# Ten more weight pairs as seven block products in a gated FFT + GEGLU kernel

## The chip, the cores and the metric

The kernel runs on one NeuronCore of a Trainium2 chip. A core has five engines that run their own instruction streams in order: PE (TensorE, matmuls), DVE (VectorE), ACT (ScalarE), POOL (GpSimd) and SP (SyncE). Transfers are issued from SP's and POOL's streams and run on 16 DMA engines. The metric is the device time of the one core in microseconds (us).

## The reference

The input is one sequence of 2048 tokens with 576 features. Two branches are mixed by a gate that is one number per token:

```python
g = sigmoid((x * gate_w).sum(-1, keepdims=True))
a = irfft2(rfft2(A_x) * (w_r + 1j * w_i))        # over tokens and features
h = gelu_tanh(B_x @ w_gate) * (B_x @ w_up)       # 576 -> 4608
b = h @ w_down                                   # 4608 -> 576
out = g * a + (1 - g) * b
```

All is float32. In the drawn inputs A_x and B_x hold the same values, so that the kernel reads one x.

## The kernel before, in words

**GEGLU branch.** Tokens are taken in two halves of 1024, and the 4608 hidden features in 36 blocks of 128; two blocks are a pair, so that there are 2 x 18 = 36 pairs to do. The matmul type is the reduced-precision float32r; to keep accuracy every operand is split into a high part (a rounded copy, made by ACT) and a low part (value minus high, made by DVE), and a product is the sum of high x high, low x high and high x low.

In the convolution form ("c", the functions `chain` and `hidden`) a block times 512 tokens is a chain of 14 matmuls of 512 columns: four feature slices of three matmuls (lines 726 to 728) and two for the last, stacked slice (lines 732 and 733). Gate and up weights make two chains, ACT takes gelu of the first, DVE multiplies by the second, and the result is split (`hb`).

In the block-product form ("s", the function `products`) a pair of blocks times 1024 tokens is treated as a 2 x 2 block product and computed with seven block products instead of eight (the Strassen-Winograd scheme). The x side is summed and split once (`operands`, into the tiles `sx` and `s4`). On the weight side four quarter blocks are loaded (`load_b`), subtracted by DVE (line 949) and split (`prep_b`, line 957). Each product is two groups of seven matmuls of 512 columns (`seven`, lines 972 to 975). DVE adds the products (line 1007) before gelu and multiplication.

In both forms the down projection (`down_mm`, line 787) has 12 matmuls of 288 columns for 128 tokens and a pair, 96 per pair and half. ACT evicts each sum, scaled by 1 - g, into one of four staging tiles (`put`, line 812), and POOL adds it to the DRAM rows `yd` with an accumulating transfer (line 800).

**Spectral branch.** The 2-D transform is done beside this, almost all on DVE: row transforms along the 576 features for each half (`forward_rows`: nine-point step, three radix-4 stages, twiddles), token transforms between tiles (`first_tiles`), the column stage (`columns`) with its own matmuls of 290 columns, the filter, and the way back (`last_tiles`, `inverse_rows`). The scaled rows are accumulated into `yd` by POOL. The 16 spectral tiles fill one large tile `til` (37 KB a partition); the operands `sx` use the same place once the tiles are gone.

**Order.** Each engine's order is written out by the program. After each half chain, each group of seven and each down sum, `gap()` is called: it issues what has fallen due (`at(n, ...)` puts a step n gaps later, `seq` a row of such steps, `due` forces the rest of a row out before its result is used), then one entry of the start list `aux`, and then steps of the spectral generator as long as a credit is positive. Matmuls raise the credit by their estimated time times `RATE` (`tick`), DVE steps lower it by their estimated duration, and a step that yields `None` ends the gap. So the spectral work is spread over the matmuls at the pace of the credit.

The 36 pairs are: 18 c pairs for the first half; for the second half five c pairs and then 13 s pairs, once the inverse transform is over and `operands` is done. Chains write to two PSUM banks (`pgu`); the column stage holds two others (`pf2`), which become `pone` for the s pairs.

Of the kernel before, what the change touches and what calls it, by code (L numbers as in the profile page):

```python
# [29 lines left out]
RATE = 1.02  # L30
STEP = 6
FIRST = 5
# [125 lines left out]
def _build(nc, tc, a):  # L158
    with ExitStack() as ctx:
# [3 lines left out]
        spec = ExitStack()  # L163
        psf = spec.enter_context(tc.tile_pool(name="psf", bufs=1, space=bass.MemoryType.PSUM))
# [12 lines left out]
        til = mk("til", [16 * SW])  # L177
        gu = [mk(f"gu{i}", [2, KT, 256], F32R) for i in range(3)]
        dn = [mk(f"dn{i}", [2, D], F32R) for i in range(4)]
        raws = mk("raws", [2 * (KT * 256 + D)])  # L180
        raw = [raws[:, i * (KT * 256 + D):(i + 1) * (KT * 256 + D)] for i in range(2)]
        hb = [mk(f"hb{i}", [2, TB], F32R) for i in range(3)]
        gl = [mk(f"gl{i}", [TB]) for i in range(2)]
        xraw = mk("xraw", [4, TB])
        stg = [mk(f"stg{i}", [2, HD]) for i in range(4)]
        tmp = mk("tmp", [2 * UNIT + 112])
        sgn = tmp[:, 2 * UNIT + 112 - KF:]
# [4 lines left out]
        cns = mk("cns", [4, NK])  # L192
        misc = mk("misc", [2 * SW])
        gwb = misc[:, 0:D]
# [9 lines left out]
        def ps_f2():  # L204
            return psf.tile([P, 2, 512], F32, name="pf2", tag="pf2", bufs=1)

        ps7 = []

        def ps_one():
            return ps7[0].tile([P, TB], F32, name="pone", tag="pone", bufs=2)  # L210
# [9 lines left out]
        st = [til[:, SW * i:SW * (i + 1)] for i in range(16)]  # L220
# [9 lines left out]
        def columns():  # L230
# [5 lines left out]
            Z = [st[q] for q in turn]  # L236
            flat = xraw.rearrange("p q k -> p (q k)")
            sp, gw, xg = flat[:, 0:SW], flat[:, SW:SW + D], flat[:, 1280:1280 + D]
# [30 lines left out]
            def product(d, kb, h, l):  # L269
                v = ps_f2()  # L270
                c = cc(d, kb).rearrange("p (a l k) -> p a l k", a=2, l=2)
                for al in range(2):
                    for n, (q, x) in enumerate(((0, h), (1, h), (0, l))):
                        pe.matmul(v[:, al, :NK], c[:, al, q], two(x)[:, al], start=n == 0, stop=n == 2)  # L274
# [6 lines left out]
            def gates():  # L281

                nc.sync.dma_start(gw, a["gw"][0:1, :].to_broadcast([P, D]))
                for t in range(8):
                    n = count[0]
                    at(2, lambda t=t: nc.sync.dma_start(xg, a["xg"][t]))
                    while count[0] < n + 7:
                        yield None
                    gate_sum(8 + t, xg, xg, gw)
                    yield 1.33  # L290
                gate_part(1, None)[1]()

            def beside():

                more = gates()
# [3 lines left out]
                for d in range(3):  # L299
                    while gone[0] < (4 * d + 5) * STEP + 5:  # L300
                        yield next(more, None)
                    yield from four(d, range(4), sp, 1)
                yield from more
# [18 lines left out]
            for kb in range(18):  # L322
# [5 lines left out]
                def filter_start():  # L328
                    vec.tensor_tensor(zi, v[:, 0, :NK], zr, ALU.subtract)
                    vec.tensor_tensor(zr, v[:, 0, :NK], zr, ALU.add)  # L330
# [10 lines left out]
                for g in range(STEP):  # L341
# [9 lines left out]
                    elif g == 1:  # L351
                        if on:
                            copy(zr, v[:, 1, :NK])
# [14 lines left out]
                    elif g == 4:  # L368
                        if was:
                            w = product(1, kb - 1, yh, yl)  # L370
                            copy(two(Z[kb - 1]), w[:, :, :NK])
# [19 lines left out]
        T = til.rearrange("p (e d k) -> p d e k", d=4, e=4)  # L391
        re, im = slice(0, NK), slice(NK, SW)

        def four(d, at, sp, sgn):

            yield from _butterfly(vec, lambda i: T[:, d, i], lambda i: T[:, d, i, re], lambda i: T[:, d, i, im],
                                  at, sp, sgn, (0.76, 0.45))

        def first_tiles(h):

# [5 lines left out]
                                  TAKEN, sp, -1, (1.37, 0.76))  # L406
            places = [((k, TAKEN[o]), o * k) for k in range(1, 4) for o in range(1, 4) if TAKEN[o] // 2 == h]
            yield from _twiddles(vec, act, lambda d, e: T[:, d, e], lambda d, e: T[:, d, e, re],
                                 lambda d, e: T[:, d, e, im], places, tmps, -1, 0.5)
            yield None  # L410

        def last_tiles():

# [6 lines left out]
                                 lambda d, e: T[:, d, e, im], places, tmps, 1, 0.5)  # L420
            yield None
            yield from _butterfly(vec, lambda i: T[:, i], lambda i: T[:, i, :, re], lambda i: T[:, i, :, im],
                                  range(4), sp, 1, (2.6, 1.35))
# [6 lines left out]
        def nine(ops):  # L430
            for o, x, c, z in ops:
# [8 lines left out]
                yield 0.45 if z is None else 0.72  # L440
# [827 lines left out]
```

## Time and profile before

| | |
|---|---|
| Three timed runs | 1386.92, 1387.72, 1387.68 us; median 1387.68 |
| Profiled execution | 1385.35 us, span 1383.5 us, granted TensorE clock 0.999 |
| Busy in the span | PE 1370.6, DVE 1038.4, ACT 752.7, POOL 266.1 us |
| DMA | 211.16 MB, mean 153 GB/s |

The profile page gives busy time per engine, the span in 40 slices (a digit is tenths of a slice), DMA queues, the chain of work that ended last, and groups of instructions by line. "PEld" is TensorE's weight load, which overlaps its matmuls. A wait row has: who waited <- for whom: total us, times, longest us. A group row has busy time and mean ns of one instruction, then the engine's idle time before them and what ended it. A row of a DMA issue has KB and the median time from issue to landing. Durations of matmuls overlap, since they are pipelined; their pace is read from the distance of their starts.

### The profile page before, as it was taken

Reading aid. Unit: us, or ns where it says so; the run is one execution under the profiler, and the core shown is the slowest. Engines: PE = TensorE matmul, PEld = TensorE weight load, DVE = VectorE, ACT = ScalarE, POOL = GpSimd, SP = SyncE. Lnnn points to the kernel's source line nnn. Section 1 sums busy time; section 2 is a strip of 40 time slices with the busy share of each in tenths; the row PEclk is TensorE's granted clock in tenths of the full one; section 3 lists DMA queues with packets and bytes.
Section 4 is the critical chain, followed back from the end, with each engine's and each line's share of the span. In section 5 each row is a group of like instructions: output and inputs, shape, how many; then the busy total and the mean of one; then the engine's idle time right before and its main releaser. Section 6 shows DMA issues by size and latency. Waiting matters only on the chain.

```text
span 1383.5 us, 19831 instructions
## 1 busy us (share of the span) xinstructions
PE 1370.6 (99%) x7504; PEld 1208.1 (87%) x7504; DVE 1038.4 (75%) x1440; ACT 752.7 (54%) x1215; POOL 266.1 (19%) x326
## 2 busy tenths in 40 slices
PE   8999999999999999999999999999999999999998
PEld 7888888888888888888888888888888888888888
DVE  5999899989878877799988997546555555555554
ACT  5553443444566575543456344866666666666662
POOL 0022111222222221111113012321112222221111
PEclk9999999999999999999999999999999999999999
DMA  7466666657899998556678467956677666766767
GB/s 269 144 123 115 154 121 122 115 100 172 207 248 268 253 256 177 103 106 117 144 140 184 117 143 136 205 81 162 131 131 132 130 129 128 132 130 130 131 138 180
DMA packets 97328, 211.16 MB, mean 153 GB/s; under 512 B 11856, under 2 KB 22096, under 8 KB 96848
## 3 DMA queue, kind: packets, MB, share of 16 engines
q0 software_dynamic: 45248, 92.56, 44.3%
q1 hardware_dynamic: 51984, 117.34, 27.0%
q8 instruction: 59, 0.97, 0.3%
q14 instruction: 37, 0.30, 0.1%
HBM read 110.69 MB, written 92.01 MB: 147 GB/s over the span
## 4 chain that ended last, share of the span: by engine, by line
PE 84%; issue 7%; DVE 4%; DMA 2%; POOL 1%; ACT 1%; SPq 1%; DVEq 0%; POOLq 0%; ACTq 0%
PE pdn L787 28%; PE pgu L726 10%; PE pgu L728 9%; PE pgu L727 9%; PE pgu L973 3%; PE pgu L972 3%; PE pgu L974 3%; PE pone L972 3%; PE pone L973 3%; PE pone L974 3%; PE pgu L732 2%; PE pgu L733 2%; PE pgu L975 2%; PE pf L274 2%; PE pone L975 1%
## 5 line engine op out<-in xcount | busy, mean ns | idle before, releaser
L800 POOL DMA_DIRECT2D yd<-stg x264 | 229.6, 871 | 1047.5 <-ACT stg L812 777.4
L787 PE MATMUL pdn<-dn,hb 128*128 128x288 f32 x2892 | 413.0, 295 | 0.0
L787 PEld LDWEIGHTS pdn<-dn,hb 128*128 128x128 f32 x2892 | 402.0, 188 | 11.8 <-DVE hb L773 0.2
L812 ACT ACTIVATE stg<-pdn,omg 128x576 f32<-128x576 f32 x272 | 201.7, 742 | 370.1 <-PE pdn L787 364.4
L726 PE MATMUL pgu<-xhi,gu 128*128 128x512 f32 x728 | 285.0, 392 | 5.0 <-DVE gl L768 3.4
L728 PE MATMUL pgu<-xlo,gu 128*128 128x512 f32 x728 | 284.0, 390 | 0.0
L727 PE MATMUL pgu<-xhi,gu 128*128 128x512 f32 x728 | 283.7, 390 | 0.0
L726 PEld LDWEIGHTS pgu<-xhi,gu 128*128 128x128 f32 x728 | 136.7, 188 | 31.4 <-DVE gl L768 5.0
L728 PEld LDWEIGHTS pgu<-xlo,gu 128*128 128x128 f32 x728 | 136.7, 188 | 29.8
L727 PEld LDWEIGHTS pgu<-xhi,gu 128*128 128x128 f32 x728 | 136.6, 188 | 24.5
L213 ACT ACTIVATE hb<-gl 128x512 fp32r<-128x512 f32 x102 | 64.0, 628 | 114.4 <-DVE gl L768 114.1
L213 ACT ACTIVATE gu<-raws 64x256 fp32r<-64x256 f32 (+3 forms) x121 | 101.6, 850 | 7.2 <-DMA raws<-wgu 5.7
L768 DVE TENSOR_TENSOR gl<-gl,pgu 128x512 f32<-128x512 f32 x92 | 62.9, 683 | 44.9 <-PE pgu L733 44.4
L764 ACT ACTIVATE gl<-pgu 128x512 f32<-128x512 f32 x91 | 54.3, 597 | 72.4 <-PE pgu L733 72.1
L787 PE MATMUL pdn<-dn,gu 128*128 128x288 f32 x540 | 83.6, 295 | 0.2 <-DVE raws L841 0.2
L787 PEld LDWEIGHTS pdn<-dn,gu 128*128 128x128 f32 x540 | 76.7, 188 | 1.9 <-DVE raws L841 0.5
L773 DVE TENSOR_TENSOR hb<-gl,hb 128x512 fp32r<-128x512 f32 x92 | 63.1, 686 | 16.5 <-ACT hb L213 16.5
L732 PE MATMUL pgu<-xtl,gu 128*128 128x512 f32 x182 | 70.9, 389 | 0.0
L733 PE MATMUL pgu<-xtl,gu 128*128 128x512 f32 x182 | 70.8, 389 | 0.0
L706 DVE TENSOR_TENSOR gu<-raws,gu 128x1280 fp32r<-128x1280 f32 x44 | 65.4, 1486 | 5.3 <-ACT gu L213 5.2
L706 DVE TENSOR_TENSOR dn<-raws,dn 128x576 fp32r<-128x576 f32 x72 | 54.1, 752 | 1.3 <-ACT dn L213 1.3
L92 DVE TENSOR_TENSOR rows<-rows 128x1280 f32<-128x1280 f32 x36 | 53.5, 1487 | 0.5
(232 smaller groups left out, 2137.0 us busy)
## 6 DMA issues: line engine op xcount, KB each, us to landing
yd<-stg POOLq DMA_DIRECT2D x264, 288.0 KB, 5.1
raws<-wgu SPq DMA_DIRECT2D x44, 640.0 KB, 5.0
raws<-wd SPq DMA_DIRECT2D x72, 288.0 KB, 3.2
colm<-col POOLq DMA_DIRECT2D x32, 256.0 KB, 6.3
raws<-ws SPq DMA_DIRECT2D x21, 384.0 KB, 6.6
quads<-ws SPq DMA_DIRECT2D x20, 384.0 KB, 6.8
tmp<-wf SPq DMA_DIRECT2D x16, 290.0 KB, 5.6
cns<-til SPq DMA_DIRECT2D x64, 72.5 KB, 5.1
```

The source lines that it names most:

```text
L213: act.activation(o, i, AF.Copy)
L706: vec.tensor_tensor(g[:, 1], r, f(g[:, 0]), ALU.subtract)
L726: pe.matmul(ps, w[:, 0, k, c], xhi[tb][:, k], start=k == 0, stop=False)
L727: pe.matmul(ps, w[:, 1, k, c], xhi[tb][:, k], start=False, stop=False)
L728: pe.matmul(ps, w[:, 0, k, c], xlo[tb][:, k], start=False, stop=False)
L732: pe.matmul(ps, w[:, 0, 4, c], xtl[tb], start=False, stop=False)
L733: pe.matmul(ps, w[:, 1, 4, c], xtl[tb], start=False, stop=True)
L787: pe.matmul(ps[half], h[:, l, c], d[:, q, half * HD:(half + 1) * HD], start=part == 0 and n == 0, stop=part == 1 and n == 2)
L800: pl.dma_start(yd[u], o, accum_op=ALU.add)
L812: put(u, lambda o: act.activation(o.rearrange("p (c k) -> p c k", c=2), v[:, :, 0:HD], AF.Copy, scale=omg[:, u:u + 1]), i == 0)
L972: pe.matmul(ps, hi, xh[:, t], start=start and t == 0, stop=False, skip_group_check=True)
L973: pe.matmul(ps, lo, xh[:, t], start=False, stop=False, skip_group_check=True)
```

## The change

The order of the pairs becomes a plan: 2 c, 10 s, 6 c for the first half, 5 c and 13 s for the second. So 23 pairs are block products instead of 13, in both halves, and what they need must exist twice.

- `operands` is called for each half. `sx` and the spectral tiles `til` take turns in one buffer: x, then `sx` of the first half, then `til` during the 11 c pairs, then `sx` of the second half. `s4` moves to a weight tile.
- While `sx` is there the rows of only one half fit in SBUF. Forward rows of half 0 are stored to DRAM (`fw`) and come back when the tiles exist; after the column stage the rows of half 1 are stored (`bw`) and come back for the last transform.
- The forward row transforms run in the first ten s pairs, the tile and column work in the c pairs, the inverse row transforms in the last 13 s pairs. `until` holds the generator for a phase; at the start of each s stretch the program issues gaps without matmuls until the operands are done, and before the last pair until the generator has ended.
- The weight quarters use five fixed places in turn instead of two sets of four; all are loaded from SP. The differences (`total`) are issued apart from the splits.
- Chains alternate between the banks `pgu` and `pone`, except in the column stage, which then uses `pone`. One more pair of hidden tiles comes from a tile `hx`.
- The credit has rate 1.0 instead of 1.02, a cap of 1.2 instead of 3.0, smaller charges for most DVE steps, and some charges are made at issue of the whole row of steps. The gates of half 1 are taken beside the first forward transform; sigmoid is written with tanh. Rows leave the inverse transform one by one. POOL's descriptor scratch is set to 4096 bytes.

```diff
-RATE = 1.02
+RATE = 1.0
 STEP = 6
-FIRST = 5
+PAIRS = NT // 2
+PLAN = "c" * 2 + "s" * 10 + "c" * 11 + "s" * 13
+PLACES = ((0, 1, 2), (2, 0, 1), (1, 2, 0))
...
+        fw, bw = (dram.tile([P, ROWS], F32, name=n, tag=n) for n in ("fw", "bw"))
...
-                yield 0.45 if z is None else 0.72
+                yield 0.36 if z is None else 0.61
...
-            yield from _butterfly(vec, *v, at, sp, sgn, (1.5, 0.82))
+            yield from _butterfly(vec, *v, at, sp, sgn, (1.41, 0.74))
...
+        def into_rows(h):
+
+            T = tile_view()
+            rows = rows_tile()
+            R = row_view(rows)
+            pl.memset(rows.rearrange("p (c k) -> p c k", c=2)[:, :, 8 * KF:], 0.0)
+            yield from moved(lambda t, c: (R[:, c, t, 0:KF], T[:, 8 * h + t, c, 0:KF]))
+            box[0] = rows
...
         def inverse_rows(h):
-            rows = rows_tile()
-            T, R = spread(h, rows)
...
+            rows = box[0]
...
+            todo_t = list(range(8))
+            n = 0
+            while todo_t:
+                t = min(todo_t, key=lambda t: abs(count[0] - added[8 * h + t] - 11)) if h else todo_t[0]
+                o = out_rows[n % 4]
+                n += 1
+                todo_t.remove(t)
+                act.activation(o, R[:, t, 0:D], AF.Copy, scale=gs[:, 8 * h + t:8 * h + t + 1])
+                at(2, lambda t=t, o=o: pl.dma_start(yd[8 * h + t], o, accum_op=ALU.add))
+                for _ in range(1 if n < 5 and h == 0 else 3):
+                    yield None
...
+        def until(n):
+            while phase[0] < n:
+                yield None
 
         def spectral(rows):
-            yield from forward_rows(0, rows)
+            yield from operands(0)
+            yield from with_gates(forward_rows(0, rows))
+            nc.sync.dma_start(fw, rows)
             rows = rows_tile()
             load_rows(rows, 1)
-            zero_pads(0)
+            for _ in range(9):
+                yield None
+            yield from forward_rows(1, rows)
+            yield from until(2)
+            til[0] = pool.tile([P, 16 * SW], F32, name="til", tag="til")
+            yield from into_tiles(1, rows)
+            rows = rows_tile()
+            nc.sync.dma_start(rows, fw)
+            yield from first_tiles(1)
+            yield from into_tiles(0, rows)
+            yield from first_tiles(0)
+            cols[0] = True
+            yield from columns()
+            cols[0] = False
+            yield from last_tiles()
+            load_xs(1, 0)
+            load_xs(1, 1)
+            yield from into_rows(1)
+            nc.sync.dma_start(bw, box[0])
             yield None
...
-            yield from columns()
-            yield from last_tiles()
-            for h in range(2):
-                yield from inverse_rows(h)
+            yield from into_rows(0)
+            yield from operands(1)
+            yield from until(3)
+            yield from inverse_rows(0)
+            box[0] = rows_tile()
+            nc.sync.dma_start(box[0], bw)
+            for _ in range(5):
+                yield None
+            yield from inverse_rows(1)
...
-            credit[0] = min(credit[0], 3.0)
+            credit[0] = min(credit[0], 1.2)
...
+        def bank():
+
+            turns[0] += 1
+            return ps_gu() if cols[0] or turns[0] // 2 % 2 else ps_one()
...
+        def load_b(q, n):
+            if q < len(PLAN) and PLAN[q] == "s":
+                nc.sync.dma_start(spots(q)[(0, 1, 3, 4)[n]], a["ws"][block(q, n // 2), n % 2])
...
-            seq(("b", i, m), (lead, total), (lead + 2, high), (lead + 4, low), (lead + 5, tail))
+            credit[0] -= 0.88
+            seq(("b", q, m), (lead + 1, high), (lead + 3, low), (lead + 4, tail))
...
+        for q, m in enumerate(PLAN):
+            current[0] = q
+            if q in starts:
+                while ops.get("done") != starts.index(q):
+                    credit[0] = 1.0
+                    gap()
+                phase[0] = 2 * starts.index(q) + 1
+            elif q and m == "c" and PLAN[q - 1] == "s":
+                phase[0] = 2
+            if q == len(PLAN) - 1:
+                while gens:
+                    credit[0] = 1.0
+                    gap()
+                for u in range(8):
+                    nc.sync.dma_start(a["y"][u], yd[u])
+            (conv if m == "c" else products)(q)
+        finale()
```

In `products` the order of the pieces within a pair is the same (seven products, down sums between them): weight loads for the next pair are issued after its second, third and fourth product, splits three products ahead of their use.

More of the change, by code (lines that the diff above doesn't have):

```diff
@@ L370, in columns @@
                             w = product(1, kb - 1, yh, yl)
[L371 removed]
+                            for al in range(2):
+                                copy(two(Z[kb - 1])[:, al], w[al][:, :NK])
                         if on:
@@ L814, in down, with pop @@
             gap()
+        def pop(n):
+            for _ in range(n):
+                if pend:
+                    d, t = pend.pop(0)
+                    down(d, t)
+                    if t == 3:
+                        spare.extend(u for _, u, _ in d[3])
+        pend = []
         def held(u):
-            return st[8 + u][:, 0:D]
+            return st(8 + u)[:, 0:D]
         def release(u):
```

582 lines of the change are left out of this document (292 added, 290 removed).

## Prediction

> **What bounds the kernel now.** I read the page first, then the busy time by stretches, the chain of waits, TensorE's waits, and DVE's instructions in order of time.
>
> ```profile
> span 1383.5 us, 19831 instructions
> PE 1370.6 (99%) x7504; PEld 1208.1 (87%) x7504; DVE 1038.4 (75%) x1440; ACT 752.7 (54%) x1215; POOL 266.1 (19%) x326
> DVE  5999899989878877799988997546555555555554
> ```
>
> TensorE is busy for all but 12.9 us of the span. DVE is near full in two thirds of the 40 slices and half idle in the last third, where the 13 block-product pairs run. The profiled execution took 1385.35 us (span 1383.5), 2.33 below the median of the three timed runs, 1387.68. I sum against 1385.35 and add 2.33 at the end.
>
> The chain of waits names the same group of 24 down matmuls twice in each pair. Its starts give the length of a pair, first for four convolution-form pairs ("c"), then for eleven product pairs ("s"):
>
> ```profile
> 183.41 3.18 PE pdn L787 x24
> ...
> 336.26 3.18 PE pdn L787 x24
> ...
> 965.28 3.18 PE pdn L787 x24
> ...
> 1351.24 3.18 PE pdn L787 x24
> ```
>
> A c pair takes (336.26 - 183.41) / 4 = 38.21 us, an s pair (1351.24 - 965.28) / 11 = 35.09 us. The same two stretches by engine (length, then PE, PEld, DVE, ACT, POOL, clock, DMA share, GB/s):
>
> ```profile
> 183.41:336.26 152.85, 152.85 (x835) 135.01 (x834) 137.44 (x185) 67.67 (x106) 30.10 (x37) 1.00 0.63 119
> 965.28:1351.24 385.96, 385.96 (x2137) 341.19 (x2136) 224.13 (x297) 240.20 (x418) 76.22 (x88) 1.00 0.69 130
> ```
>
> In both TensorE never rests and has full clock, so a matmul removed there is time removed. DVE is 90% busy in the first, with spectral work between the pairs; in the second, with an s pair's own work alone, 58% (20.4 us a pair). That free 42% is what the change wants to use.
>
> TensorE's waits, all that reach 0.4 us:
>
> ```profile
> PE pgu L726 <- DVE gl L768: 3.4, 3, 2.0
> PE pgu L726 <- ACT gl L761: 1.6, 1, 1.6
> PE pgu L1100 <- DVE gate L1096: 1.5, 1, 1.5
> PE pgu L745 <- DVE xhi L1106: 0.8, 1, 0.8
> ```
>
> **The change, part by part.**
>
> *Matmuls.* The plan string has 2 c, 10 s, 11 c and 13 s pairs: ten pairs turn from c to s. By the code a c pair has 8 chains of 14 matmuls of 512 columns, an s pair 7 products of 2 x 7, so 112 become 98. By the two spacings that is 10 x (38.21 - 35.09) = **-31.2 us**, all on TensorE's path.
>
> *DVE's ledger.* The spectral work is handed out by credit: matmuls earn (98 x 0.2265 + 96 x 0.131 = 34.8 in an s pair, 37.9 in a c pair), DVE work spends. The new charges are smaller than the old, 0.61 for 512 columns where the old had 0.72, 1.41 for 1280 where it had 1.5. DVE's order of time shows whether they are real:
>
> ```profile
> 209.91 0.69 DVE L435 TENSOR_TENSOR tmp<-rows 128x512 f32<-128x512 f32 x1
> 210.63 0.69 DVE L437 TENSOR_TENSOR rows<-rows 128x512 f32<-128x512 f32 x1
> 211.24 0.68 DVE L435 TENSOR_TENSOR tmp<-rows 128x512 f32<-128x512 f32 x1
> ...
> 220.51 1.49 DVE L92 TENSOR_TENSOR tmp<-rows 128x1280 f32<-128x1280 f32 x1
> 221.92 0.68 DVE L768 TENSOR_TENSOR gl<-gl,pgu 128x512 f32<-128x512 f32 x1
> ```
>
> An instruction lasts 0.69 us, but the next starts 0.61 us after it (210.63 to 211.24), or 0.72 where it reads what was just written (209.91 to 210.63). For 1280 columns it is 1.41. So the charges are the true pace of independent instructions; dependent ones run 0.11 over. About every second of the 31 instructions of the inverse nine-point step is such a one, and one or two in a stage: some 28 of its 94, so 28 x 0.11 = 3 us on 70 charged, 4%.
>
> An s pair charges 19.6 of its own: seven splits and four differences of weights at 0.88, six adds 3.7, four hidden blocks 4.9, two dn splits 1.4. That leaves 15.2 for spectral work; a c pair (9.1 of its own) leaves 28.9. Now stage by stage. First ten s pairs: the first has 8, the next nine 15.2 each, together 145; both forward row transforms with the gates want 80 + 73 = 153. The rest spills into the first c pair, which nothing forbids. The eleven c pairs: 0.55 pairs of spill; two moves into tiles 0.85; two first-tile steps 1.15; the column stage about 5.3 (107 gaps of its own pace, 24 gaps a pair, and what stands around it); last tiles 1.0; two moves into rows 0.8: 9.7 pairs, with 10 there before the operands of the second half must begin. Last 13 s pairs: two inverse transforms at 70.4 and some 45 gaps of idle pacing take 12 pairs, with 12 there. It fits, but nowhere with more than a third of a pair to spare.
>
> Where DVE is handed its full credit, its demand is 34.8 + 0.04 x 15.2 = 35.4 us per s pair against TensorE's 35.09: 0.3 us a pair over, for 18 such pairs 5.7 us. A split is issued two chains or more ahead of its use (8 us), so part of that is swallowed. Ends 0 and 15 (0.8 a pair); I take **+3**, between nothing and the whole of the 5.7.
>
> *Rows through DRAM.* Four transfers of 2560 KB are new. The nearest rows:
>
> ```profile
> rows<-xn SPq DMA_DIRECT2D x2, 2304.0 KB, 11.1
> raws<-ws SPq DMA_DIRECT2D x21, 384.0 KB, 6.6
> ```
>
> By size one takes about 11.1 x 2560 / 2304 = 12.3 us (estimate). After the first forward transform the rows are stored and the other half is loaded into the same buffer, so SP waits at that load for the store, 12.3 us, and the load takes 11.1 more: 23.4 us. The kernel waits nine gaps, and a gap of an s pair is 35.09 / 22 = 1.6 us: 14.4. DVE then stands for 9 us, and behind its first waiting instruction the pair's own adds and splits are queued. The 8 us of lead swallow most; what stays is lag in a stage where DVE can't catch up. Ends 0 and 9; I take **+4**, nearer the middle, since the lag isn't worked off before the c pairs. Weight loads stand behind this on SP's queue: the ledger puts the store in the last fifth of a pair, and the next loads are issued 8 us into the following one. They land at about their time; ends 0 and 12, taken as 0.
>
> [...]
>
> After the column stage the rows of half 1 are stored and those of half 0 moved into the same buffer one gap later. ACT's first copy comes some 3 us after the store is issued and waits for its end, about 9 us; the evictions of down sums stand behind it. The trace has a smaller case, ACT with 5.33 us of copies in one piece at 735, where TensorE waited the 2.0 us of the first wait row above:
>
> ```profile
> 735.42 5.33 ACT L580 ACTIVATE til<-rows,gs 128x576 f32<-128x576 f32 x4
> ```
>
> So about 3.3 us were swallowed with two banks for the chains. Now the chains have four outside the columns, two more chains of 3.2 us. Ends 0 (all swallowed) and 6 (9 - 3.3); I take **+3**. The burst itself goes, since rows now leave one by one: **-2**.
>
> The other two transfers: the load of the stored forward rows has 22 us of tile work before it is read (0). The last load has five gaps, 8 us, against 12.3; DVE stands for 4, within the lead (ends 0 and 4, taken 0).
>
> *Deadlines.* At each c-to-s change the program issues gaps without matmuls until the operands are done. Their generator needs about 27 gaps by its pauses and 18.6 us of charges at 1.2 a gap, and the pair before has 24 (the first time 23). The last three or four are issued at once: a few splits and eight 32-row copies, used only by the third product, 8 us on. Ends 0 and 6 each; **+1** each. The end rush before the last pair, at worst two row copies of the kind that took 5.33 / 4 = 1.3 us: **+1** (ends 0 and 4).
>
> *Costed at nothing.* The ACT work added (seven splits and seven 64-row copies a pair) has cover: ACT was busy 240.2 of 385.96 us in s pairs. Two 290-column copies instead of one in columns, the gates' loads moved to the first s pairs and tanh in place of sigmoid are ACT and SP work with the same cover; without it they cost under 3 us. The smaller descriptor scratch for POOL's transfers shows nowhere; by POOL's row (19% busy) even twice the issue time stays below the pairs' pace.
>
> Sum: 1385.35 - 31.2 + 3 + 4 + 3 - 2 + 2 + 1 = 1365.2; on the scale of the median 1367.5, so **1367**.
>
> **The rivals.**
>
> *All is covered.* Every new wait lies inside its lead: 1387.7 - 31.2 - 2 = 1354.5. For it: in 152.85 us with DVE 90% busy TensorE did not wait once. Against it: the full demand was under DVE's pace there, and it is over now.
>
> *SP's queue is the price.* If the forward transform ends in the first half of a pair, the weight loads of the next pair stand behind 23.4 us of rows. The first is used by ACT 9.5 us after issue and lands in 6.6 now; it would come 10 to 14 us late, and ACT's evictions behind it. That adds some 11 us to the forecast: 1378. Where the store falls hangs on the ledger, which I trust to 0.3 of a pair. [...]
>
> *The operands come late.* The c stage overruns by half a pair, and 12 gaps of operand work are issued with no matmul beside them, 10 us: 1377.
>
> *Slower: DVE sets the pace of s pairs.* In s pairs DVE now waits for ACT:
>
> ```profile
> DVE hb L995 <- ACT hb L213: 34.5, 19, 2.2
> DVE gl L991 <- ACT gl L999: 16.1, 13, 1.3
> DVE gu L995 <- ACT gu L213: 14.4, 7, 3.5
> DVE gu L957 <- ACT gu L213: 10.1, 25, 1.2
> ```
>
> That is 75.1 us over 13 pairs, 5.8 a pair. If half of it stays when DVE has no slack, each of 18 filled pairs is 2.9 us longer, 52 us: 1367 + 52 - 3 = 1416. It decides from (1387.7 - 1367.5 + 3) / 18 = 1.3 us a pair. Against it: DVE waits there because it runs ahead of the ACT copy that is issued with the matmuls; with work to do it comes later, and in the stretch at 183 no such wait reached TensorE.
>
> **How the numbers follow.** Forecast 0.55 (its own range 1358 to 1375), all covered 0.22, SP's queue 0.12, late operands 0.04, DVE's pace 0.07. A measurement of this kernel tells 0.2%, 2.8 us, from no change. Slower is the last rival, 0.07; same is the upper edge of the two before it, 0.03; faster 0.90. The range reaches down to the covered case with a little below, 1353, and up past SP's queue, 1382; the slower rival stays outside it.
>
> **What would show it.** Pairs of 35.1 us in 23 places and 14 matmuls of 512 columns fewer in each of ten pairs show the first term. TensorE waits of 2 to 6 us near 290 us (the store and load of rows) and near 800 (ACT waiting for the store of rows) show the next; none there means the covered case. S pairs of 35.4 to 36 with spectral work beside them show the ledger; above 36.4 the slower rival. Weights landing over 15 us after issue show SP's queue. I am wrong if TensorE's idle time outside start and end is over 30 us, or if the columns run into the last 13 pairs.

## The result

| | before | after |
|---|---|---|
| median of the runs | 1387.70 us | 1376.39 us (1374.25, 1377.17, 1376.51, 1376.27) |
| profiled execution, span | 1385.35, 1383.5 us | 1374.25, 1372.5 us |

The ratio is 0.9916, with an interval of 0.9899 to 0.9933. The change makes the kernel faster by 11.3 us, 0.8%; the forecast was 1367, a gain of 20.7, and its range (1353 to 1382) holds the time. So the sign is right, and nearly half of the expected gain went somewhere. These are the page's first rows for the kernel after, with DVE's and the clock's rows of the 40 slices:

```profile
span 1372.5 us, 20070 instructions
PE 1344.1 (98%) x7364; PEld 1186.9 (86%) x7364; DVE 1142.8 (83%) x1605; ACT 846.9 (62%) x1444; POOL 263.2 (19%) x322
...
DVE  7689999989999768867786587689989779989854
...
PEclk9999999999999999999999999989999999999999
```

TensorE has 140 matmuls fewer, and DVE is now 8 or 9 tenths full in most slices of both s stretches (4 to 13 and 27 to 38), where it had been half idle in the second. But TensorE stands for 28.4 us (1372.5 - 1344.1), where it stood for 12.9. The down groups of the chain of waits give the pairs as before, two starts of each stretch:

```profile
180.43 3.18 PE pdn L835 x24
215.48 3.18 PE pdn L835 x24
...
486.35 3.18 PE pdn L835 x24
524.56 3.18 PE pdn L835 x24
...
1106.01 3.18 PE pdn L835 x24
...
1316.33 3.18 PE pdn L835 x24
```

An s pair takes 35.05 us in the first half (215.48 - 180.43) and in the second (210.32 / 6), a c pair 38.21: the pace of the kernel before, in every stretch that isn't disturbed. So the pairs did what the first term says, and the loss lies in single places. TensorE's waits name them:

```profile
PE pgu L1044 <- ACT sx L214: 6.6, 1, 6.6
PE pone L1041 <- DVE xraw L1077: 3.7, 2, 2.6
PE pone L276 <- DVE colm L269: 2.8, 1, 2.8
PE pgu L1041 <- DVE xraw L1077: 2.4, 2, 1.6
PE pgu L1041 <- ACT gl L214: 1.9, 1, 1.9
```

To price a place fully I added up, over the matmul records in order of time, how far each start lies behind the one before it beyond the undisturbed step (0.2275 us for 512 columns, 0.1326 for 288, 0.1335 for 290). This holds a wait and the slow matmuls after it. Before, the sum is 16.1 us, after it is 36.9. With 140 x 0.2275 = 31.85 us of matmuls gone, 31.85 - 20.8 = 11.0 us should be gained, and the two profiled executions differ by 11.1.

| place, us | what TensorE waits for | lost before | lost after |
|---|---|---|---|
| start, to 16 | first loads and splits | 6.5 | 6.3 |
| 102 to 121 | DVE behind, first change from c to s | - | 5.1 |
| 699 to 707 | a column operand, at the reload of x | - | 4.7 |
| 888 to 912 | operands of the second half, second change | - | 12.1 |
| 924 to 940 | DVE behind, after the second change | - | 4.65 |
| 1094 | hidden block | - | 1.4 |
| single waits before, 742 the largest (2.25) | | 7.1 | - |
| end, and pieces under 0.3 | | 2.5 | 2.65 |

Of 28 us of new losses 21.85 stand at the two changes from c to s, where the prediction had put 2.

### The profile page after: what moved, and what is told of

The parts are those of the page before. It is cut to its first block, busy times and chain, and to the rows that moved or that the text cites. A ratio compares the mean times of both kernels' runs of the same rounds, so it can differ in the third digit from the quotient of the medians.

```text
span 1372.5 us, 20070 instructions
## 1 busy us (share of the span) xinstructions
PE 1344.1 (98%) x7364; PEld 1186.9 (86%) x7364; DVE 1142.8 (83%) x1605; ACT 846.9 (62%) x1444; POOL 263.2 (19%) x322
## 4 chain that ended last, share of the span: by engine, by line
PE 85%; DVE 6%; ACT 4%; DMA 2%; issue 2%; SPq 0%; DVEq 0%; ACTq 0%
PE pdn L835 30%; PE pgu L1041 5%; PE pgu L1043 5%; PE pgu L1042 5%; PE pone L1041 5%; PE pgu L760 5%; PE pgu L762 5%; PE pgu L761 4%; PE pone L1043 4%; PE pone L1042 4%; PE pgu L1044 2%; PE pone L1044 2%; PE pone L760 2%; PE pone L762 2%; PE pone L761 2%
## 5 line engine op out<-in xcount | busy, mean ns | idle before, releaser
L214 ACT ACTIVATE gu<-wq 64x256 fp32r<-64x256 f32 (+4 forms) x353 | 228.5, 666 | 101.7 <-DVE gu L1006 90.9
L1006 DVE TENSOR_TENSOR gu<-wq,gu 128x768 fp32r<-128x768 f32 x161 | 153.5, 953 | 18.9 <-ACT gu L214 18.5
L835 PE MATMUL pdn<-dn,hx 128*128 128x288 f32 x876 | 134.2, 295 | 0.2 <-DVE wq L899 0.2
L835 PEld LDWEIGHTS pdn<-dn,hx 128*128 128x128 f32 x876 | 124.9, 189 | 4.1 <-DVE wq L899 0.5
L760 PE MATMUL pgu<-xhi,gu 128*128 128x512 f32 x300 | 117.9, 393 | 0.0
L762 PE MATMUL pgu<-xlo,gu 128*128 128x512 f32 x300 | 117.8, 393 | 0.0
L761 PE MATMUL pgu<-xhi,gu 128*128 128x512 f32 x300 | 117.7, 392 | 0.0
L1023 DVE TENSOR_TENSOR wq<-wq 128x768 f32<-128x768 f32 x92 | 87.7, 953 | 7.9 <-ACT gu L214 7.9
L762 PEld LDWEIGHTS pgu<-xlo,gu 128*128 128x128 f32 x300 | 56.6, 189 | 12.3
L760 PEld LDWEIGHTS pgu<-xhi,gu 128*128 128x128 f32 x300 | 56.8, 189 | 9.9
L761 PEld LDWEIGHTS pgu<-xhi,gu 128*128 128x128 f32 x300 | 56.7, 189 | 9.9
L1044 PE MATMUL pgu<-sx,gu 128*128 128x512 f32 x138 | 54.5, 395 | 6.6 <-ACT sx L214 6.6
L1041 PE MATMUL pgu<-xhi,gu 128*128 128x512 f32 x140 | 55.6, 397 | 2.5 <-DVE xraw L1077 2.4
L1041 PE MATMUL pgu<-sx,gu 128*128 128x512 f32 x140 | 55.7, 398 | 1.9 <-ACT gl L214 1.9
L1043 PE MATMUL pgu<-sx,gu 128*128 128x512 f32 x140 | 55.2, 395 | 0.0
```

The source lines that it names most:

```text
L214: act.activation(o, i, AF.Copy)
L760: pe.matmul(ps, w[:, 0, k, c], xhi[tb][:, k], start=k == 0, stop=False)
L761: pe.matmul(ps, w[:, 1, k, c], xhi[tb][:, k], start=False, stop=False)
L762: pe.matmul(ps, w[:, 0, k, c], xlo[tb][:, k], start=False, stop=False)
L835: pe.matmul(ps[half], h[:, l, c], d[:, k, half * HD:(half + 1) * HD], start=part == 0 and n == 0, stop=part == 1 and n == 2)
L1006: vec.tensor_tensor(o, x.rearrange("p (c k) -> p c k", c=3), f(w[:, 256:1024]).rearrange("p (c k) -> p c k", c=3), ALU.subtract)
```

## The experiments

Each edit is against the kernel after, or against the experiment named. The times are medians with the ratio to the kernel before in the same set of runs. Where the text says "in the program's order", gaps and matmuls are counted in the order in which the program issues them (a c pair has 24 gaps); 22.5 pairs then means the middle of the pair with number 22, counted from 0.

**The rows through DRAM** (price in the prediction: 4 + 3). The two stores and the two loads of rows are left out, so that the spectral branch works on the rows of the wrong half in places:

```diff
-            nc.sync.dma_start(fw, rows)
...
-            rows = rows_tile()
-            nc.sync.dma_start(rows, fw)
...
-            nc.sync.dma_start(bw, box[0])
...
-            box[0] = rows_tile()
-            nc.sync.dma_start(box[0], bw)
```

> The four row transfers through DRAM are left out (the rows in the buffer are used in their place, so that the spectral branch computes with the rows of the wrong half); every other instruction is the same. By the prediction's steps the store and load and the store before the move into rows cost 4 + 3 us, so 1369. By the trace of the changed kernel, where no TensorE wait stands near 290 us and the one at 1094 us is 1.3 us, they cost 0 to 2: 1374 to 1376.5, a little lower if the move into rows, no longer waiting for the store, also brings the operands forward.

Measured: 1376.38 us, ratio 0.992 (0.9904 to 0.9937), against 1376.39 with the transfers. TensorE's longest wait is the same to the tenth:

```profile
PE pgu L1038 <- ACT sx L214: 6.6, 1, 6.6
```

So the four transfers cost nothing that these runs can tell (the interval is 2 us wide to each side), and the table above has no loss near 290 or 858 us, where they stand. The trace of the kernel after shows how. SP's queue at the first turn (start, length), then the groups of transfer issues with KB and time to landing:

```profile
279.58 0.33 SPq L603 DMA_DIRECT2D fw<-rows  x1
290.00 0.33 SPq L574 DMA_DIRECT2D rows<-xn  x1
293.86 10.18 SPq L991 DMA_DIRECT2D wq<-ws  x4
```

```profile
rows<-xn SPq DMA_DIRECT2D x2, 2304.0 KB, 11.2
...
fw<-rows SPq DMA_DIRECT2D x1, 2560.0 KB, 10.4
rows<-fw SPq DMA_DIRECT2D x1, 2560.0 KB, 12.7
bw<-rows SPq DMA_DIRECT2D x1, 2560.0 KB, 8.5
rows<-bw SPq DMA_DIRECT2D x1, 2560.0 KB, 12.6
```

Store and load took 10.4 + 11.2 = 21.6 us, as expected (23.4). But DVE's first instruction on the new rows waited only 0.63 us for them:

```profile
289.33 0.17 DVE L695 TENSOR_SCALAR gs<-gate 128x8 f32<-128x8 f32 x1 [2.63 <-ACT gate L694]
...
300.24 0.75 DVE L739 TENSOR_TENSOR dn<-wq,dn 128x576 fp32r<-128x576 f32 x1
301.62 0.69 DVE L426 TENSOR_TENSOR tmp<-rows 128x512 f32<-128x512 f32 x1 [0.63 <-DMA rows<-xn]
```

In DVE's queue the pair's own splits, adds and hidden blocks stand before it, with 5.4 us of waits among them, the longest the one for the gate (2.63). The prediction counted the nine gaps as TensorE's time from the store on. In the program's order 1478 matmuls stand before the store, and TensorE reached that place at 287.0; but DVE was ahead of TensorE there and done with the rows at 279.5, so the store left 7.4 us earlier. The first read stands ten gaps after the store, which TensorE reached at 303.0. So the transfers had 22 us, not 14.4.

**The reload of x.** In the column stage the kernel loads and splits x again for the second token half (`reload_x`). Here that is left out, and the second half computes with the first half's x:

```diff
-                    for k in range(3):
-                        load_x(k)
+                    pass
                 if (q, tb) in ((PAIRS - 1, 1), (PAIRS, 0)):
-                    reload_x(1 - tb)
+                    pass
```

> The reload of x for the second token half is left out (its ten loads and the splits on ACT and DVE; the second half then computes with the x of the first); all else as in the changed kernel. Theory R (the 4.7 us lost at 699 us come from the reload's splits, which fall into the column stage, where a column product follows DVE by two gaps): the loss there falls under 0.5, time 1371 to 1373. Rival (the column stage with two chain banks and its own dense steps has this wait anyway): it stays above 3 us, and 1376.

Measured: 1369.85 us, ratio 0.988 (0.9866 to 0.9895), 6.5 us less than after by the medians and 5.0 by the two ratios; that is 1.2 us below the span of theory R. The 4.7 us at 699 to 707 are gone and the losses at 883 to 912 stay. The order of DVE around 700 in the kernel after says why:

```profile
697.43 0.75 DVE L739 TENSOR_TENSOR dn<-wq,dn 128x576 fp32r<-128x576 f32 x1
698.10 1.48 DVE L739 TENSOR_TENSOR gu<-wq,gu 128x1280 fp32r<-128x1280 f32 x1
699.50 0.48 DVE L218 TENSOR_SCALAR tmp<-tmp,msk 128x512 f32<-128x512 f32 x1
700.02 0.75 DVE L219 SCALAR_TENSOR_TENSOR xtl<-xtl,msk,tmp 128x512 fp32r<-128x512 f32 x1
...
701.55 0.75 DVE L269 TENSOR_TENSOR colm<-tmp,colm 128x580 fp32r<-128x580 f32 x1
```

Two splits of weights and the two instructions for the stacked slice of x stand ahead of the column operand that the matmul at 702.36 waits for. (The edit takes out the loads and ACT's copies as well; that the order on DVE is what counts is borne out further down, where larger charges for the same splits alone, with a debt at the changes, bring this loss to 0.3.) The prediction had no term for it: the kernel before reloads x in the same way and loses nothing there, as its column stage ran at another place beside it (from 357 to 550 us; after, from 566 to 780).

**Fewer pauses in the moves.** The moves between rows and tiles pause after each second token step instead of each:

```diff
-                yield None
+                if t % 2:
+                    yield None
```

> The four moves between rows and tiles pause after every second token step instead of after each, 16 gaps fewer in the c stretch, 25 us of lead for the operands of the second half; their copies are unchanged. Theory A (the operands come half a pair late because the c stretch is paced by pauses, and TensorE pays for their work at the second change to products): the waits between 885 and 940 us fall from 16 us to under 6, and the time from 1376.4 to 1364 to 1368. Rival B (the operands' own ACT and DVE work costs this at any change, early or late): within 3 us of 1376.4, the waits only move.

Measured: 1373.94 us, 0.9907 (0.9892 to 0.9922): 2.5 us less than after, with intervals that overlap, and not the time that was expected. The 16 gaps that the expectation counts on were not saved: in the program's order the first move takes 11 gaps instead of 12, since a gap also ends when the credit is used up, and the first operand step of the second half comes at 22.54 pairs instead of 22.63 (it may come at 22.0). The place at 889 to 909 still costs 9.1 us. The pauses of the moves didn't hold it.

**One more c pair.** The plan has 12 c pairs in the middle and 12 s pairs at the end:

```diff
-PLAN = "c" * 2 + "s" * 10 + "c" * 11 + "s" * 13
+PLAN = "c" * 2 + "s" * 10 + "c" * 12 + "s" * 12
```

> One pair of the last stretch goes back to the convolution form (12 c and 12 s at the end instead of 11 and 13): 3.1 us more of matmuls, one pair of lead for the operands. Theory A: the second change loses its 16 us down to about 5, so 1366 to 1370. Rival B: 1379 to 1380, the matmuls alone. A third possibility: the last stretch is now too short for the inverse transforms and the rush before the last pair takes 5 us or more of the gain.

Measured: 1393.94 us, 1.005 (1.0035 to 1.0065). As a time this tells little: with twelve c pairs the turn of the weight tiles puts `s4` and the last c pair's weights into one tile. That kernel computes with wrong operands, and waits for splits of weights in the last stretch (10.4 us at 961 the longest). Two places can be read all the same. The one around 911 fell to 1.1 us, as a later deadline should make it. And 13.5 us went at 1334 to 1350, ahead of the last pair, which is the rush of the third possibility: in the program's order 27 gaps without matmuls stand there, where the kernel after has 10, and ACT makes eight row copies in one run.

**A debt at the changes.** The credit starts each s stretch at -8, so that DVE first does the pair's own work:

```diff
+                credit[0] = -8.0
```

(after the loop that issues the operands' gaps)

> At the start of each product stretch the credit is set to -8, so that no spectral step is issued for some 12 gaps. Theory L (the waits at 105 to 120 and 924 to 940 us, 4.6 and 4.2 us, are DVE's lag from the operands issued in one piece, which the full credit never lets it work off): both vanish, 1367 to 1370; the direct wait for the operands at 888 us stays. Rival (they come from ACT or from weights that land late): within 2 us of 1376.4.

Measured: 1379.11 us, 0.9949 (0.9932 to 0.9967); the ten runs go from 1376.32 to 1386.69, and the traced one is the slowest of them. The median is 2.7 us above the kernel after, not the 6 to 9 below it that theory L expected. The waits for `xraw`, 3.7 + 2.4 us after the changes, are gone. So that part of the loss was DVE's queue, filled with spectral steps when the products' adds became due. But what is put off is paid later:

```profile
PE pgu L1041 <- ACT gl L214: 10.4, 2, 8.5
PE pgu L1044 <- ACT sx L214: 9.5, 1, 9.5
```

The second row is the wait for the operands, 6.6 us before; the 8.5 us of the first stand at 1328, ahead of the last pair, when the rest of the inverse transform is issued in one piece (24 gaps in the program's order).

**The cap of the credit.** The change lowered the cap from 3.0 to 1.2 beside the charges. A gap of a half chain earns 7 x 0.2265 = 1.59 on average, and what is above 1.2 is thrown away. Here the c pairs have 3.0 again:

```diff
-            credit[0] = min(credit[0], 1.2)
+            credit[0] = min(credit[0], 3.0 if PLAN[current[0]] == "c" else 1.2)
```

> The credit's cap is 3.0 in c pairs (as in the kernel before) and stays 1.2 in s pairs. By the order in which the instructions are issued the operands of the second half then stand between 0.0 and 0.5 of the last c pair instead of 0.5 and 1.0, and the column stage is over a pair earlier. Theory A' (the column and tile steps were held up because the cap throws away credit at gaps with a large charge; the lateness of the operands is what TensorE waits for at 888 to 911 us): the 12 us lost there fall under 2, those at 105 to 120 us (4.6 to 5) fall by some too, and the time is 1361 to 1366. Rival B (the lateness is not what costs; the first product pair's own splits and copies crowd ACT and DVE): within 4 us of 1376.4. Rival C: with the cap at 3.0 DVE comes in bursts, and new waits of 1 to 3 us in the column stage take back half of it: 1368 to 1371.

Measured: 1379.86 us, 0.9952 (0.9935 to 0.9969). In the program's order the operands begin at 22.0 pairs, as early as they may, and end at 22.75; in the kernel after they begin at 22.63, and their last 17 gaps have no matmul beside them. The 12.1 us at the second change are 1.0. So the cap is what made the operands late, and the lateness is what cost: rival B is out, though the time lies in its span. But the column stage now loses 1.8, 4.0, 2.4 and 2.8 us at 535, 620, 684 and 721, and 6.8 us go at 829 to 839, where the rows are stored:

```profile
DVE rows L507 <- DMA bw<-rows: 9.0, 1, 9.0
ACT rows L214 <- DMA bw<-rows: 8.3, 1, 8.3
...
PE pdn L835 <- DVE hb L821: 3.9, 1, 3.9
```

This is the wait that the prediction priced at +3. In the kernel after, ACT comes 6.4 us after the store was issued, the store takes 8.5, and ACT waits 2.1 us; here ACT comes 3.1 us after it, the store takes 11.4, ACT waits 8.3, and TensorE loses 6.8. The low cap had covered it.

**Cap, pauses and a debt of 4 together** (the edits of "The cap of the credit" and "Fewer pauses in the moves", and the debt with a credit of -4):

> The cap of 3.0 in c pairs, pauses in the moves after every second token step, and a credit of -4 at the start of each product stretch. The spectral steps end 0.7 pair before the last pair by the issue order, so that no rush comes there, unlike with -8 at 1328 us. Theory A' and L together: the waits at 105 to 120 and at 885 to 940 us, 21 us, fall under 4 in all; what stays is the column wait near 700 us (5) and the start (6): 1357 to 1361. If L is wrong, no better than the cap alone.

Measured: 1388.95 us, 1.0015 (0.9998 to 1.0033); ten runs from 1381.76 to 1394.34. The waits at the changes are down to 3.3 us in all, but the columns lose more in one place (7.3 us at 605), the store of rows costs 9.5 at 812 to 824, and 7.5 us went at 1333, ahead of the last pair, as with the larger debt. The three don't add up.

**The cap of 3.0 in c pairs, but not in the column stage:**

```diff
-            credit[0] = min(credit[0], 1.2)
+            credit[0] = min(credit[0], 1.2 if cols[0] else 3.0 if PLAN[current[0]] == "c" else 1.2)
```

> The cap is 3.0 in c pairs outside the column stage, 1.2 elsewhere. Theory: the bursts between 515 and 725 us seen with 3.0 everywhere (535, 620, 684, 721 us: 11 us) go back to the one loss at 700 us (5), while the operands are issued in time as there, so nothing is lost at 885 to 911 us. ACT still waits for the store of rows near 840 us: 3 to 7 us lost. Sum: 1376.4 - 12 - 1 + 5 = 1366 to 1371. Rival (any earlier column stage meets the same bursts): 1376 or more.

Measured: 1369.34 us, 0.9887 (0.9864 to 0.991). In the program's order the column stage begins 0.6 pairs earlier (at 14.04 instead of 14.67) and takes as long as after (145 gaps for 146); the operands come at 22.0 to 22.75, and the second change costs 1.0 at 889 and 3.5 at 920 to 935. So what this edit gains, 18 gaps up to the operands, comes from the steps ahead of the columns (15 of them). 6.0 us remain at 838 to 846, the store of rows.

**Seven gaps between that store and the next move**, beside the edit above:

```diff
             nc.sync.dma_start(bw, box[0])
-            yield None
+            for _ in range(7):
+                yield None
```

> As v1_cap_out, and seven gaps instead of one between the store of rows and the move into the same buffer. Theory S (ACT, standing 8 us at the store, is what TensorE loses near 840 us): the loss there falls under 0.5 and the time is 3 to 7 us below v1_cap_out. Rival (the loss near 840 is the moves' own ACT work): the same as v1_cap_out.

Measured: 1364.83 us, 0.9848 (0.9833 to 0.9863), 4.5 us below the version above. The loss at the store is gone; the column operand at 701 is now the largest, 7.5 us.

**Charges for the split of x that are nearer its work**, and a debt of 3 at the changes, beside the two edits above:

```diff
-                credit[0] -= 0.61
+                credit[0] -= 1.2
...
-                credit[0] -= 1.45
+                credit[0] -= 2.5
...
+                credit[0] = -3.0
```

> As v2_hold, with the reload of x charged double (1.2 and 2.5 instead of 0.61 and 1.45), so that column steps stand back for it, and a credit of -3 at the start of each product stretch. Theories R and L: the column loss near 700 us falls from 5 to under 2, the losses at 105 to 120 and 924 to 945 us from 4 to 5 each to under 2; the rush before the last pair stays away, since the spectral steps end 0.6 pair earlier by the issue order. 1356 to 1362. If charges don't move the column loss: 1361 to 1365.

Measured: 1363.09 us, 0.9832 (0.9815 to 0.9848). That is 1.1 us above the expected span. The column operand costs 0.3, the first change 2.9, the second 4.8. The rush did not stay away. What is left ahead of the last pair, in a table of the waits from 1300 to 1316 us:

```profile
PE pgu L1042 <- ACT gl L214: 5.7, 1, 5.7
...
ACT tmp L568 <- DMA yd<-tmp: 3.8, 1, 3.8
```

ACT copies finished rows into four buffers in turn and waits for the transfer that adds one to DRAM; TensorE's sum waits for ACT's eviction behind it.

**Rows of the second half leave at two gaps each instead of three**, beside all that:

```diff
-                for _ in range(1 if n < 5 and h == 0 else 3):
+                for _ in range(1 if n < 5 and h == 0 else 2 if h else 3):
```

> As v4_all, but the copies of finished rows of the second half pause at 2 gaps each instead of 3. Theory E: the 7.4 us that TensorE loses at 1309 to 1317 in v4_all come from row copies that are still owed when the last pair is due and are made in one burst; 8 gaps earlier (0.36 pair) they are done, the loss there falls under 3 us and the time to 1356 to 1360. Rival F: the copies wait for the transfers that accumulate rows, whatever the pacing; the loss stays at 5 to 8 us and the time is 1362 to 1364.

Measured: 1361.82 us, 0.9819 (0.9803 to 0.9836), between the two expectations; the loss there is 5.2 us instead of 7.4, which is in the rival's span, though in the program's order 8 gaps instead of 16 are left ahead of the last pair. TensorE's wait, and ACT's for its buffer in the stretch from 1295 to 1320:

```profile
PE pgu L1042 <- ACT gl L214: 3.4, 1, 3.4
...
ACT orow L568 <- DMA yd<-orow: 2.9, 1, 2.9
```

So ACT still waits for a buffer's return. That pacing is the other part isn't shown: the two medians differ by 1.3 us, their intervals overlap, and 7.4 and 5.2 are one trace each. The median of this version is 14.6 us below the kernel after.

## Why the prediction was right, and where it wasn't

*Matmuls, -31.2:* right. 35.05 us for an s pair in both halves, 140 matmuls fewer, 31.85 us.

*DVE's ledger, +3 for drift:* nothing of it. In a stretch of the ten s pairs with everything beside them, DVE is full and TensorE never waits (length, then PE, PEld, DVE, ACT, POOL, clock, DMA share, GB/s):

```profile
240.00:280.00 40.00, 40.00 (x226) 35.61 (x225) 39.86 (x47) 24.63 (x43) 8.63 (x10) 0.95 0.68 122
```

From 125 to 690 us no single place loses 0.3 us. The row shows busy time, whose rows overlap, so that 39.86 of 40 isn't proof of demand above pace; the loss is the measure, and it is none. The reading behind the term was wrong as well. The instruction at 210.63 doesn't read what the one at 209.91 wrote (`tmp`); it writes over rows that the other one reads. In the two forward transforms of the kernel before, the 35 neighbours of this kind start 0.72 us apart (0.715 to 0.728), and the 11 in which the second writes over nothing that the first reads 0.60 to 0.61.

*Forward rows, +4; backward rows, +3; SP's queue as rival:* the first store and load took about the time that was worked out, 21.6 us, but the runs without the transfers are no faster. The failed step in the first is "DVE then stands for 9 us": it took 14.4 us from the store to the read, which were 22, since DVE was 7.4 us ahead of TensorE at the store, and DVE stood 0.63. In the second the step was right in mechanism, and in size a matter of who is early: 2.1 us of ACT's wait after, none of which reached TensorE, and 8.3 with the higher cap, with 6.8 us lost by TensorE.

*ACT's burst of rows, -2:* right in size, the 2.25 us at 742 are gone. The other single waits of before, 4.9 us in sum, are gone too; no term counted them, and no run shows why they went.

*Deadlines, +1 and +1:* this is the term that failed. At the two changes 5.1 and 16.8 us were lost. Two steps are wrong. The first is the ledger of the c stretch, "9.7 pairs, with 10 there". It counted 28.9 us of spendable credit in every c pair and set the new cap of 1.2, which the change lists, at nothing. These are its stages in gaps, 24 to a pair, beside the program's order in three kernels:

| stage | ledger | after, cap 1.2 | 3.0 in c pairs outside the columns | 3.0 in all c pairs |
|---|---|---|---|---|
| rest of the forward rows | 13 | 15 | 13 | 13 |
| two moves into tiles | 20 | 23 | 20 | 20 |
| two first-tile steps | 28 | 30 | 20 | 20 |
| columns | 127 | 146 | 145 | 134 |
| last tiles | 24 | 23 | 24 | 23 |
| two moves into rows | 19 | 22 | 19 | 19 |
| sum | 231 | 259 | 241 | 229 |

With a cap of 3.0 the sum holds to 2 gaps, by errors that cancel (the columns 7 too short, the first-tile steps 8 too long); with 1.2 it is 28 gaps too small, 19 of them in the columns, and the ten pairs that were there have 244 (the first c pair has 28). (The first row, 0.55 pairs, divides 8 us by what an s pair leaves, 15.2; by a c pair's 28.9 it would be 7 gaps.) So in the kernel after the operands come 0.6 pairs late, and 17 of their gaps are issued with no matmul beside them, where the prediction had three or four. With the cap at 3.0, outside the columns as well as everywhere, none is, and the 12.1 us fall to 1.0, so this is shown. The second is "a few splits and eight 32-row copies, used only by the third product". As the operands were late, ACT got all of their copies in one piece when the second half began:

```profile
892.93 0.61 ACT L214 ACTIVATE gu<-xraw 128x512 fp32r<-128x512 f32 x1
893.68 2.56 ACT L214 ACTIVATE sx<-xraw 32x512 fp32r<-32x512 f32 x4
...
900.92 3.84 ACT L214 ACTIVATE sx<-xraw 32x512 fp32r<-32x512 f32 x6
904.78 1.58 ACT L214 ACTIVATE gu<-wq 128x768 fp32r<-128x768 f32 x2
```

A copy of 32 rows takes 0.64 us (2.56 / 4), as long as one of 128 rows (0.61); with 14 of these and 12 of 128 rows from 889 to 905 ACT was behind for both the operands and the evictions. The 5.1 us at the first change and 4.65 after the second are DVE's queue, as the debt shows, with which both are gone. The prediction had no term for DVE's lag there. Operand steps that are left over aren't its cause at the first change: with the cap of 3.0 in c pairs none is left there, and 4.2 us still go.

*End rush, +1:* nothing was lost there, although the sum behind it was loose. Two inverse transforms and 45 gaps make 11.3 pairs by the ledger's own figures (140.8 / 15.2 + 45 / 22), where it says 12; in the program's order they take 12 pairs and 10 gaps without matmuls before the last pair.

*The rivals.* "The operands come late", half a pair, 12 gaps, 10 us, 1377, is what happened at the second change: the operands are 0.6 pairs late, 17 gaps stand without matmuls, the place costs 12.1 us, and the median is 1376.4. It had a chance of 0.04, since the ledger was trusted to a third of a pair. That the two totals agree so well is luck: the terms that weren't there (3 + 4 + 3 + 1 = 11) stand against losses that weren't foreseen (5.1 + 4.7 + 4.65 + 1.4 = 15.85), less the waits of before that went beside the 2 counted (5.1). *All covered* is out by the waits; *DVE sets the pace* is out, 35.05 us a pair; *SP's queue* didn't come up: its condition was a transform that ends in the first half of a pair, and in the program's order it ended one gap before the end of one. The weight tiles' loads in the stretch from 285 to 312 us, behind the rows, landed so after their issue:

```profile
DMA to landing us min/median/max: 3.9/6.0/10.2
```

None took the 15 us that were set as its sign. The first of them fits a place behind the rows: the rows were issued at 290.00 and landed at 301.6, these weights were issued at 293.86 and landed at 304.0, the 10.2 us of the line, where the median of all 92 such loads is 4.2.

*What was set as a sign of being wrong,* over 30 us of TensorE's idle time outside start and end or columns in the last 13 pairs, didn't come: of the 28.4 us in the page, 20.2 lie between 16 and 1360 us, and the column matmuls end at 780.

## What to carry to other kernels

When work is handed out by a credit, the cap on the credit is a part of the supply: count what can be spent, not what is earned, and do it stage by stage. At a change of stage look at the one engine that gets everything at once (ACT with 26 copies here), not at the mean share of engines. And when a wait goes, ask which work had been hidden by lateness: the higher cap brought up the store of rows that the low one had covered.

## What the runs showed of the hardware

**Around three of its waits TensorE was granted half its clock.** The wait of 2.85 us ends at 702.36, and seven matmuls later the starts lie 0.43 us apart instead of 0.23, for eight matmuls:

```profile
703.46 0.41 PE L762 MATMUL pgu<-xlo,gu 128*128 128x512 f32 x1
703.69 0.61 PE L766 MATMUL pgu<-xtl,gu 128*128 128x512 f32 x1
704.09 0.63 PE L767 MATMUL pgu<-xtl,gu 128*128 128x512 f32 x1
```

The stretches by granted clock show it as 0.50 exactly there, and again at 895 and 908.7 us:

```profile
703.69:706.65 2.96, 2.96 (x8) 2.28 (x7) 2.84 (x5) 1.77 (x5) 0.35 (x1) 0.50 1.07 270
...
895.00:898.00 3.00, 3.00 (x7) 2.42 (x8) 2.53 (x4) 2.93 (x5) 0.00 (x0) 0.50 0.00 0
908.70:911.30 2.60, 2.60 (x8) 2.01 (x7) 2.60 (x4) 0.53 (x2) 0.87 (x1) 0.50 0.52 37
```

Each time costs some 8 x 0.2 = 1.6 us beside the wait, 4.8 us in the kernel after. In the clock's record the three stretches go from 703.61 to 707.03, from 891.35 to 898.17 and from 908.41 to 911.83 us, which is 3.41, 6.83 and 3.41 us; the second begins within the wait of 6.63 us that ends at 895.00. The wait before the third was 1.94 us, while a wait of 2.62 us at 105 was followed by full pace. The same wait in the kernel with twelve c pairs was followed by half pace (the first line is the kernel after, the other two are that kernel):

```profile
107.95 0.50 PE L1041 MATMUL pone<-xhi,gu 128*128 128x512 f32 x1 [2.62 <-DVE xraw L1077]
...
107.65 0.56 PE L1041 MATMUL pone<-xhi,gu 128*128 128x512 f32 x1 [2.63 <-DVE xraw L1077]
108.00 0.63 PE L1042 MATMUL pone<-xhi,gu 128*128 128x512 f32 x1
```

So the length of the wait alone doesn't decide. The edges of the three stretches lie whole multiples of 3.413 us apart, 1, 55, 57, 60 and 61 times that behind the first. What makes the clock fall isn't shown.

**A granted clock of 0.95 cost nothing.** In the profiled execution after, the record stands at 0.95 in the first s stretch and, from 1015 us on, at 1.00 in the second (columns as above):

```profile
180.27:215.32 35.05, 35.05 (x196) 31.11 (x194) 33.02 (x56) 25.33 (x50) 6.91 (x8) 0.95 0.71 139
...
1100.00:1200.00 100.00, 100.00 (x552) 88.53 (x551) 92.07 (x110) 66.52 (x115) 23.31 (x27) 1.00 0.81 175
```

A pair takes 35.05 us in both, and the profiled execution, with a mean of 0.958, is the shortest of the four (1374.25 us; the others have 0.992 to 0.994). So here a difference of 5% in the recorded clock isn't one of pace; only the halves are.
